# An FFT convolution with routed experts on one core: 48-point stages of groups 1 and 2 that are asked for sooner

## The chip, the core and the metric

The kernel runs on one core of a Trainium2 chip. A core has five engines with a program each, run in order: TensorE (PE; its weight loads are PEld), VectorE (DVE), ScalarE (ACT), GpSimd (POOL) and SyncE (SP), which issues most DMAs. An engine waits for another by semaphores, and what stands behind a waiting instruction on its engine waits too. 16 DMA engines move the data. The metric is the time of the device in microseconds; lower is better.

## The reference

`x` is 8 sequences of 5696 tokens of 128 numbers. Each channel is convolved causally with a filter `h` as long as the sequence (by a Fourier transform in the reference), and every token of the result goes to the one expert of eight with the largest logit:

```python
Yf = np.fft.rfft(x, n=2 * S, axis=1) * np.fft.rfft(h, n=2 * S, axis=0)[None]
y = np.fft.irfft(Yf, n=2 * S, axis=1)[:, :S, :].reshape(B * S, D)
logits = y @ w_gate
expert = np.argmax(logits, axis=1)
gate = softmax(logits)[expert]
for e in range(8):
    out[expert == e] = gate * (relu(y[expert == e] @ w1[e]) @ w2[e])
```

## The kernel before

**The convolution** is a transform in two factors: 119 points, padded to 120, by 48 points. The eight sequences go in three groups of 2, 3 and 3 (group 0, 1, 2), and each group passes three stages. Stage A (`steps_a`) makes the first factor: matmuls `pa`, copied to `ut` and stored to a buffer `VU` in DRAM. Stage B (`phase_b`), the 48-point stage, runs 120 items: an item is a forward matmul `xp`, a product with the filter's transform on VectorE (three instructions, `zt` and `xs`), a sum on GpSimd, and an inverse matmul `vp`, copied to `vt` and stored back to `VU`. Four items are a block, and a block needs four loads on SyncE: `mt` (forward matrices), `uq` (from `VU`, so all of stage A must be stored), two `mi` (inverse matrices) and two `hh` (filter). Blocks are asked for two ahead. Stage C (`phase_c`) makes the second factor (`yp`), transposes (`tp`), computes logits and gates (`lp`, `gb` and a chain of short VectorE instructions) and ranks tokens; GpSimd then sorts them by expert into a buffer `SR` with indirect DMAs. While group g is in stage C, group g+1's stage A runs as its guest.

**The experts** (`pipeline`) work on 185 tiles of 256 sorted tokens in four parts; part 0 has 26 tiles, part 1 has 33. A tile has four steps: in each a first-layer group `mh` of six matmuls, a ReLU `hs` on ScalarE and VectorE, and, two steps later, a second-layer group `ma`. A tile's tokens come as rows `xr` from `SR` and are transposed into `mx`; its weights come in four pieces `wb_0` to `wb_3` from `WD`. A piece is loaded in fact only where the expert changes, and in parts 0 and 1 there is one set of buffers, so a new expert's `wb_0` can only be loaded when the tile before has done with it. Rows are asked for by `usable(t)`, which wants the part sorted and the flag `state["alone"]` off; weights by `known(t)`, which wants the part's table.

**The order** of each engine's program comes from `run`: the streams (convolution, weight preparation, experts) are generators that yield a planned cost in ns, and the stream with the smallest planned time emits next. `STEP` (1420) is the planned cost of one expert step. `MIX_B`, `MIX_C`, `BESIDE` and `ENDING` say how many expert steps go with one item of stage B and one sub-step of stage C; `ENDING[g]` is that of the sub-steps after the last synthesis. In group 0 no experts run yet while `alone` is on. `next(after)` lets the next group's stage B emit its next piece: its first two pieces are requests of a block, further ones are items. `spin(n)` emits n filler matmuls on TensorE.

Of the kernel before, what the change touches and what calls it, by code (L numbers as in the profile page):

```python
# [49 lines left out]
MIX_B = (0.0, 0.45, 0.85)  # L50
MIX_C = (1.0, 1.2, 2.2)
BESIDE = (1.4, 1.2, 2.2)
ENDING = (1.4, 2.5, 2.5)
KNOWN = 2840
STAGED = 64
PAIRED = 2
# [3 lines left out]
HOLD = 3  # L60
FETCHED = (0, 1)
GUESTED = (0,)
EAGER = (2, 0)
SETTLED = (2840, 8000, 8000)
LEAD = (0, 4, 6)
A3 = (True, True, True)
# [4 lines left out]
LOGIT = (2, 2, 2)  # L71
RARE = 3
XR = 7
SPIN = (22, 40, 24)


@with_exitstack
def conv_moe(ctx: ExitStack, tc: tile.TileContext, I, out, B, S, D, E, F, split):
# [73 lines left out]
    groups, parts = [], []  # L152
# [74 lines left out]
    def spin(count):  # L227
        bank = ps.tile([P, 512], F32, tag="cx", name=f"spin{spun[0]}", bufs=4)
        spun[0] += 1
        for k in range(count):  # L230
            nc.tensor.matmul(
                bank, fcr[:, 0, 0], fcr.rearrange("p a c q -> p (a c q)"), start=True, stop=True
            )
# [220 lines left out]
    def phase_b(gr, guest=None):  # L454
# [139 lines left out]
        if g == 0:  # L594
            spin(SPIN[0])
        for qb in range(2 if g == 0 else 0):
# [42 lines left out]
    state = {"w9": [const.tile([MP, max(SLOTS), E1], F32, name=f"w9{k}") for k in range(2)]}  # L639
# [51 lines left out]
    def phase_c(gr, guest=None, after=None):  # L691
        g, nb, cb, cw, NI, ns = gr.g, gr.nb, gr.scb, gr.scw, gr.ni, gr.ns
# [9 lines left out]
        nu = NB // NI  # L702
# [16 lines left out]
        def bank(name, tag):  # L719
            return ps.tile([P, 512], F32, tag=tag if state["alone"] else "cx", name=name, bufs=banks[tag] if state["alone"] else 4)  # L720
# [178 lines left out]
        finished, ahead = [None], [0]  # L899
# [4 lines left out]
        for n in range(n_end + 1):  # L904
            for k in range(nsub):
                at = n * nsub + k
                if parts[0].ready and state["prepped"]:
                    state["alone"] = False
                if k == 0:
                    load(n + 2)  # L910
                made = turning = read = carried = None
                if n < nu:
                    made = synth(n, k)
                if TL <= at < total_sub + LL:
                    tp = bank(f"tp{g}_{n}_{k}", "ma")
                if 0 <= at - TL < total_sub:
                    turning = turn(*divmod(at - TL, nsub), tp)
                whole = 0 <= at - LL < total_sub and (at - LL) % nsub == nsub - 1
                if whole:
                    for j in range(nsub):  # L920
                        spare = tp if j else ybank.get((n, k))
                        if spare is None:
                            spare = bank(f"lp{g}_{n}_{k}", "mh")
                        read = logit((at - LL) // nsub, j, spare)
                if k == 0 and n >= sl:
                    score(n - sl, n - sl - 1)
                if guest:
                    few = n < QUIET[g] or k == 0 and n >= sl and not state["alone"] and g
                    carried = guest.begin(1 if few else 2)
                ties = [made, read, carried] if carried and read else [made, turning, read or carried]  # L930
                ties = [x for x in ties if x is not None]
                count = 3 if len(sorts) > 8 else PER_SUB[g]
                for x in ties if len(ties) <= count else ties[:1] + ties[len(ties) - count + 1 :]:
                    sort_one(x)
                if state["alone"]:
                    yield cost if n < nu else cost / 2
                else:
                    yield STEP * (BESIDE if n < nu else ENDING)[g]
                if guest:
                    guest.end()  # L940
                    if guest.m >= guest.M and not guest.over and guest.done():
                        finished[0] = at
                if finished[0] is not None and at >= finished[0] + 4 and n >= nu - EAGER[g] and ahead[0] < 2:
                    next(after)
                    ahead[0] += 1
                if n < nu:
                    divide(*divmod(at + AHEAD, nsub))
                    settle(n, k)
                if 0 <= at - TL < total_sub:
                    turned(*divmod(at - TL, nsub))  # L950
                for j in range(nsub if whole else 0):
                    logit_out((at - LL) // nsub, j)
                if k == 0:
                    chains = []
                    if 0 <= n - sl - 1 < nu:
                        chains.append(rank(n - sl - 1))
                    if 0 <= n - sl < nu:
                        chains.append(route(n - sl))
                    zipped(*chains)
                    if n - sl - 1 in closes:  # L960
                        pt = closes[n - sl - 1]
                        chores.append(tables(pt, state["base"]))
                        if pt is parts[-1]:
                            chores.append(fill(pt, state["base"]))
                chore(3 if state["alone"] is False else 10)
                if at >= total_sub + LL:
                    break
        if guest:
            if not guest.over:
                yield from guest.rest()  # L970
            state["spare"] = g > 0
        state["alone"] = False
        more = True
# [129 lines left out]
    def home(t):  # L1103
        return seq[t][1] % sets(t)
# [159 lines left out]
    def pipeline(lo, hi):  # L1264
        LAG = 2
        step, nrow, nw, turned = (lo, 0), lo, (lo, 0), lo
        seen, hist, passed = {}, [None] * (LAG + 1), {}
        while True:
            t, k = step
            while nw[0] < min(t + 3, hi) and known(nw[0]):  # L1270
                was, n = user[nw[0]], nw[1]
                if home(nw[0]) and not state["spare"]:
                    break
                if was is not None and was >= lo and passed.get((was, n // 2), -1) < 2 * (n % 2) + 1:
                    break
                load_w(nw[0], n)
                nw = (nw[0], n + 1) if n < 3 else (nw[0] + 1, 0)
            while nrow < min(t + 4, hi) and usable(nrow):
                load(nrow)
                seen[nrow] = len(hist)  # L1280
                nrow += 1
            act = step if t in xts and nw > (t, k // 2) else None
            hist.append(act)
            old, done = hist[-1 - LAG], hist[-2 - LAG]
            to = done[0] if done and done[1] == NPAIR - 1 else None
            ti = turned if turned < nrow and seen[turned] + 2 <= len(hist) else None
            if ti is not None and (act and k < LAG or ti > t + 1 or act is None and ti > t):
                ti = None
            if act is None and old is None and to is None and ti is None:
                state["acting"] = False  # L1290
                leave(len(hist))
                recall(len(hist))
                deliver()
                if t >= hi and not (any(hist[-1 - LAG :]) or pending or leaving or staged or coming or returned):
                    return
                busy = pending or leaving or staged or coming or returned or turned < nrow or any(hist[-1 - LAG :])
                yield STEP if busy else None
                continue
            leave(len(hist))
            recall(len(hist))  # L1300
            if act and step == (0, 0):
                spin(SPIN[2])
            if act:
                layer1(t, k)
                state["acting"] = True
                passed[t, 0] = k
            if ti == 0:
                spin(SPIN[1])
            if to is not None or ti is not None:
                turn(to, ti)  # L1310
            if old:
                layer2(*old)
                passed[old[0], 1] = old[1]
            yield STEP
            done = None
            if act:
                done = relu(t, k)
                step = (t, k + 1) if k < NPAIR - 1 else (t + 1, 0)
                if k == NPAIR - 1:
                    xts.pop(t)  # L1320
            if ti is not None:
                turned_in(ti)
                turned += 1
            if old and old[1] == NPAIR - 1:
                drain(old[0])
            if to is not None:
                emit(to, len(hist))
            deliver(done)
# [140 lines left out]
```

## Time and profile before

| | us |
|---|---|
| median of 3 runs (2144.11 to 2147.92) | 2147.75 |
| the profiled execution, its own time | 2146.88 |
| its span, first to last instruction | 2145.2 |
| TensorE busy in the span | 2052.4 (96%) |
| VectorE busy | 1556.4 (73%) |
| GpSimd busy | 1264.6 (59%) |
| ScalarE busy | 1104.5 (51%) |

Busy shares are means over stages with different limits. Stage A and B of group 0 fill the time to some 260 us, its stage C that to some 400; experts and convolution then run together to some 1600, and experts alone from there. Matmuls are pipelined, so a few in a row start closer together than their durations say, and some matmul records are missing, which shows as idle time that no wait explains.

### The profile page before, as it was taken

Reading aid. Unit: us, or ns where it says so; the run is one execution under the profiler, and the core shown is the slowest. Engines: PE = TensorE matmul, PEld = TensorE weight load, DVE = VectorE, ACT = ScalarE, POOL = GpSimd, SP = SyncE. Lnnn points to the kernel's source line nnn. Section 1 sums busy time; section 2 is a strip of 40 time slices with the busy share of each in tenths; the row PEclk is TensorE's granted clock in tenths of the full one; section 3 lists DMA queues with packets and bytes.
Section 4 is the critical chain, followed back from the end, with each engine's and each line's share of the span. In section 5 each row is a group of like instructions: output and inputs, shape, how many; then the busy total and the mean of one; then the engine's idle time right before and its main releaser. Section 6 shows DMA issues by size and latency. Waiting matters only on the chain.

```text
span 2145.2 us, 47047 instructions
## 1 busy us (share of the span) xinstructions
PE 2052.4 (96%) x14284; PEld 1763.9 (82%) x14284; DVE 1556.4 (73%) x3731; ACT 1104.5 (51%) x2359; POOL 1264.6 (59%) x1399
## 2 busy tenths in 40 slices
PE   7899899899999999989999999999999999999998
PEld 5788666666667988876777779999989999999998
DVE  3598856699987788879988885777765555555554
ACT  5688755233334666633443345655544444554544
POOL 5366547565653388882665661788876444444443
PEclk9999999999999999999999999999999999999999
DMA  9899999799997788767889886666645543444441
GB/s 340 291 301 325 320 395 366 213 278 279 272 279 234 288 273 296 264 198 218 250 249 248 243 246 228 212 209 211 199 149 186 170 139 108 142 138 143 143 144 34
DMA packets 236901, 494.39 MB, mean 230 GB/s; under 512 B 33553, under 2 KB 146446, under 8 KB 236647
## 3 DMA queue, kind: packets, MB, share of 16 engines
q1 hardware_dynamic: 212279, 443.06, 66.2%
q0 software_dynamic: 24368, 48.29, 6.9%
q8 instruction: 116, 1.90, 0.4%
q14 instruction: 138, 1.13, 0.2%
HBM read 598.31 MB, written 176.80 MB: 361 GB/s over the span
## 4 chain that ended last, share of the span: by engine, by line
PE 29%; issue 15%; POOL 13%; DMA 6%; DVE 6%; ACT 1%; SPq 1%; POOLq 1%; DVEq 0%; ACTq 0%
PE mh L1164 9%; PE ma L1185 8%; POOL out L1240 8%; POOL SR L656 3%; PE vp L564 3%; PE xp L528 3%; PE yp L742 2%; DMA SR<-rt,pi 2%; DMA wb<-WD 2%; POOL c_fcs L650 1%; PE mx L183 1%; DVE hs L1172 1%; PE pa L315 1%; PE tp L183 1%; DMA vq<-VU 1%
## 5 line engine op out<-in xcount | busy, mean ns | idle before, releaser
L1172 DVE SCALAR_TENSOR_TENSOR hs<-mh,hs 128x512 fp32r<-128x512 f32 x728 | 501.4, 691 | 371.6 <-ACT hs L1170 366.5
L1164 PE MATMUL mh<-xtb,wb 128*128 128x256 f32 x4368 | 686.0, 293 | 27.2 <-DMA wb<-WD 12.7
L1170 ACT ACTIVATE hs<-mh 128x512 fp32r<-128x512 f32 x728 | 435.7, 599 | 449.3 <-PE mh L1164 435.4
L1164 PEld LDWEIGHTS mh<-xtb,wb 128*128 128x128 f32 x4368 | 582.8, 189 | 95.3 <-issue 34.3
L1185 PE MATMUL ma<-hs,wb 128*128 128x256 f32 x4368 | 653.7, 285 | 7.3 <-DMA wb<-WD 7.3
L1185 PEld LDWEIGHTS ma<-hs,wb 128*128 128x128 f32 x4368 | 566.9, 190 | 8.7 <-DMA wb<-WD 8.7
L656 POOL DMA_INDIRECT SR<-rt,pi x384 | 402.8, 1049 | 196.3 <-issue 55.0
L1240 POOL DMA_INDIRECT out<-xr x250 | 243.8, 975 | 316.0 <-DVE xr L1203 257.7
L555 POOL TENSOR_TENSOR zt<-zt,xs 128x384 f32<-128x384 f32 (+1 forms) x280 | 298.3, 1075 | 115.3 <-DVE xs L547 86.9
L579 ACT COPY vt<-vp 96x384 f32<-96x384 f32 (+1 forms) x300 | 149.1, 497 | 349.2 <-PE vp L564 344.4
L564 PE MATMUL vp<-zt,mi 128*96 128x384 f32 (+1 forms) x720 | 259.2, 455 | 7.2 <-DVE xs L547 5.8
L528 PE MATMUL xp<-uq,mt 96*128 96x384 f32 (+1 forms) x720 | 258.7, 454 | 4.4 <-ACT vt L579 2.3
L540 DVE TENSOR_TENSOR zt<-xp,hh 128x384 f32<-128x384 f32 (+1 forms) x300 | 174.0, 580 | 54.6 <-PE xp L528 40.6
L564 PEld LDWEIGHTS vp<-zt,mi 128*96 128x96 f32 x720 | 113.3, 163 | 100.2 <-issue 52.1
L1240 POOL DMA_INDIRECT out<-xb x114 | 111.1, 975 | 135.3 <-ACT hs L1170 111.0
L547 DVE SCALAR_TENSOR_TENSOR xs<-xp,hh 64x384 f32<-64x384 f32 (+1 forms) x300 | 175.7, 586 | 6.1
L545 DVE TENSOR_TENSOR xs<-xp,hh 64x384 f32<-64x384 f32 (+1 forms) x300 | 173.2, 577 | 6.0
L315 PE MATMUL pa<-xc,fcr 120*128 120x512 f32 x576 | 166.8, 420 | 11.0 <-ACT xc L293 4.0
L528 PEld LDWEIGHTS xp<-uq,mt 96*128 96x128 f32 x720 | 121.7, 192 | 34.7 <-issue 13.1
L315 PEld LDWEIGHTS pa<-xc,fcr 120*128 120x128 f32 x576 | 101.5, 192 | 44.5 <-DVE rk L867 7.5
L650 POOL TENSOR_TENSOR c_fcs<-c_fcs 120x64 f32<-120x64 f32 (+1 forms) x288 | 125.9, 437 | 6.2
L742 PE MATMUL yp<-vr,gcr 120*120 120x384 f32 x576 | 117.5, 338 | 1.2 <-DVE vr L730 1.1
(137 smaller groups left out, 2275.6 us busy)
## 6 DMA issues: line engine op xcount, KB each, us to landing
wb<-WD SPq DMA_DIRECT2D x728, 512.0 KB
vq<-VU SPq DMA_DIRECT2D x64, 768.0 KB
VU<-ut SPq DMA_DIRECT2D x48, 768.0 KB
uq<-VU SPq DMA_DIRECT2D x60, 576.0 KB
VU<-vt SPq DMA_DIRECT2D x60, 576.0 KB
xt<-x SPq DMA_DIRECT2D x96, 256.0 KB
xr<-SR SPq DMA_DIRECT2D x182, 130.0 KB
hh<-HS SPq DMA_DIRECT2D x120, 192.0 KB
```

The source lines that it names most:

```text
L315: done = nc.tensor.matmul(banks[m], lhs, rhs, start=(k == 0), stop=(k == len(ops) - 1))
L528: nc.tensor.matmul(xj, mt[:, k0 + j, :], uc.rearrange("p (b d) -> p b d", d=D), start=True, stop=True)
L540: nc.vector.tensor_tensor(out=zt, in0=x3, in1=hv[:, 0].broadcast_to([P] + wide), op=ALU.mult)
L547: nc.vector.scalar_tensor_tensor(out=xs[to], in0=x3[at], scalar=-1.0, in1=him, op0=ALU.mult, op1=ALU.mult)
L555: eng.tensor_tensor(out=zt, in0=zt, in1=xs, op=ALU.add)
L564: nc.tensor.matmul(vp[:K2, j * cw : (j + 1) * cw].rearrange("p (b d) -> p b d", d=D), mi[:, k0 + j, :], zt.rearrange("p b (j d) -> p b j d ...
L656: s = nc.gpsimd.indirect_dma_start(out=SR[:, :], out_offset=IndirectOffsetOnAxis(ap=pi[:, b : b + 1], axis=0), in_=rt[:, b, :], in_offset= ...
L1164: nc.tensor.matmul(hp[:, u, :], wb[:, a, f, :], xt[:, b, :], start=(n == 0), stop=(n == 2))
L1170: done = nc.scalar.activation(hs[:, 0], hp, AF.Relu)
L1172: nc.vector.scalar_tensor_tensor(out=hs[:, 1], in0=hp, scalar=0.0, in1=hs[:, 0].bitcast(F32), op0=ALU.max, op1=ALU.subtract)
L1185: nc.tensor.matmul(accs[t], wb[:, a, f, :], hs[:, b, u, :], start=(k == 0 and u == 0 and n == 0), stop=(k == NPAIR - 1 and u == 1 and n == 2),
L1240: sc = nc.gpsimd.indirect_dma_start(out=out[:, :], out_offset=IndirectOffsetOnAxis(ap=xr[:, s, D + 1 : D + 2].bitcast(I32), axis=0), in_=x ...
```

## The change

`EAGER` and the third number of `SPIN` go. In group 0's stage C, `alone` stays on until the stage ends. The next group's two block requests are made as soon as stage A of that group has ended (group 0), or one sub-step after that among the ending sub-steps (group 1); for group 0 every further sub-step then also emits an item of stage B, with 40 fillers ahead of the first. The 40 fillers ahead of tile 0's rows and the 24 ahead of tile 0's first step go. `ENDING` of group 1 is 1.4 where it was 2.5.

```diff
-ENDING = (1.4, 2.5, 2.5)
+ENDING = (1.4, 1.4, 2.5)
-EAGER = (2, 0)
-SPIN = (22, 40, 24)
+SPIN = (22, 40)
@@ phase_c, each sub-step
-                if parts[0].ready and state["prepped"]:
+                if g and parts[0].ready and state["prepped"]:
                     state["alone"] = False
...
-                if finished[0] is not None and at >= finished[0] + 4 and n >= nu - EAGER[g] and ahead[0] < 2:
-                    next(after)
-                    ahead[0] += 1
+                if finished[0] is not None and n >= nu * g and at >= finished[0] + g:
+                    if ahead[0] < 2:
+                        for _ in range(1):
+                            next(after)
+                            ahead[0] += 1
+                    elif g == 0:
+                        if ahead[0] == 2:
+                            spin(SPIN[1])
+                        ahead[0] += 1
+                        yield next(after)
...
             if not guest.over:
                 yield from guest.rest()
+            while ahead[0] < 2:
+                next(after)
+                ahead[0] += 1
@@ pipeline
-            if act and step == (0, 0):
-                spin(SPIN[2])
             if act:
                 layer1(t, k)
...
-            if ti == 0:
-                spin(SPIN[1])
```

Line numbers differ by one to nine between the two kernels. What the change does to the order shows at three places. On SyncE, where group 1's stage B begins: the last store of its stage A, and what is requested behind it. Before:

```order
L308 DMA VU_71<-ut_11_1_4309 128x1536
...
L1115 DMA xr_4467<-SR 128x260
...
L1115 DMA xr_4500<-SR 128x260
...
L1135 DMA wb_0_4511<-WD 128x1024
...
L464 DMA mt_0_4761<-mq 96x512
L472 DMA uq_0_4763<-VU_71 96x4x384
L475 DMA mi_98<-miq 48x384 x2
L479 DMA hh_95<-HS 48x1024 x2
```

And after the change:

```order
L307 DMA VU_71<-ut_11_1_4309 128x1536
L463 DMA mt_0_4439<-mq 96x512
L471 DMA uq_0_4441<-VU_71 96x4x384
L474 DMA mi_98<-miq 48x384 x2
L478 DMA hh_95<-HS 48x1024 x2
...
L1144 DMA wb_0_4569<-WD 128x1024
...
L1144 DMA wb_3_4575<-WD 128x1024
...
L478 DMA hh_97<-HS 48x1024 x2
...
L1124 DMA xr_4685<-SR 128x260
```

The first block has moved from behind the rows and weights of tile 0 to directly behind the stores; left out between `hh_95` and `wb_0` is the second block (item 4 on), between `wb_3` and `hh_97` the third (item 8 on) but for that line. The rows of tiles 0 to 3, which came first, now come behind three blocks and four weights.

On TensorE, at the same place, from the fillers on. Before:

```order
L231 MATMUL spin_4519<-fcr 128x512 x40
L183 MATMUL mxNone_4560<-ident,xr_4467 128x128 x2
L782 MATMUL lp_16_1_4596<-yt_15_4440,c_small 32x120 x3
L782 MATMUL tp_16_1_4595<-yt_15_4440,c_small 32x120 x3
L231 MATMUL spin_4609<-fcr 128x512 x24
L1164 MATMUL mh_0_4634<-xtb_4606,wb_0_4511 128x256 x6
...
L1185 MATMUL ma_4698<-hs_2_4739,wb_3_4517 128x256 x6
L528 MATMUL xp_0_0_4824<-uq_0_4763,mt_0_4761 128x384
```

And after the change:

```order
L781 MATMUL tp_16_1_4506<-yt_15_4448,c_small 32x120 x3
L230 MATMUL spin_4517<-fcr 128x512 x40
L527 MATMUL xp_0_0_4558<-uq_0_4441,mt_0_4439 128x384
...
L527 MATMUL xp_6_0_4740<-uq_4_4468,mt_4_4466 128x384
L563 MATMUL vp_2_0_4742<-zt_2_0_4661,mi_98 96x384
L182 MATMUL mxNone_4751<-ident,xr_4685 128x128 x2
L527 MATMUL xp_7_0_4763<-uq_4_4468,mt_4_4466 128x384
L563 MATMUL vp_3_0_4765<-zt_3_0_4671,mi_98 96x384
L527 MATMUL xp_8_0_4777<-uq_8_4652,mt_8_4586 128x384
L563 MATMUL vp_4_0_4779<-zt_4_0_4730,mi_99 96x384
L1173 MATMUL mh_0_4791<-xtb_4788,wb_0_4569 128x256 x6
```

Items 0 to 6 forward and 0 to 2 back now stand ahead of the transposes of tile 0's rows (`mxNone`), and items 7 and 8 ahead of its first step. The item that stood level with tile 1's first step (`xp_0`) now comes a tile and a quarter sooner in the order.

On SyncE, where group 2's stage B begins (`VU_72`). Before, the piece `wb_0` of tile 34 comes behind the first block:

```order
L1216 DMA STG<-xr_11791 128x260
L464 DMA mt_0_13172<-mq 96x512
L472 DMA uq_0_13174<-VU_72 96x4x384
L475 DMA mi_98<-miq 48x384 x2
L479 DMA hh_95<-HS 48x1024 x2
L1135 ISA
L1135 DMA wb_3_4517<-WD 128x1024
...
L1135 DMA wb_0_4511<-WD 128x1024
```

And after the change, where the pieces are those of tile 30, but for `wb_3`, which is tile 29's:

```order
L307 DMA VU_72<-ut_11_1_12235 128x1536
L1225 DMA STG<-xr_10926 128x260
...
L1144 DMA wb_3_4575<-WD 128x1024
...
L1144 DMA wb_0_4569<-WD 128x1024
L463 DMA mt_0_12662<-mq 96x512
L471 DMA uq_0_12664<-VU_72 96x4x384
L474 DMA mi_98<-miq 48x384 x2
L478 DMA hh_95<-HS 48x1024 x2
L1144 ISA
L1144 DMA wb_1_4571<-WD 128x1024
L1144 ISA
L1144 DMA wb_2_4573<-WD 128x1024
```

The first block has moved some three tiles ahead, close behind the last stores of stage A, and it now stands between the first and the second weight piece of a tile.

## Rows read from the trace of the kernel before

**Rows 1.** Stretches: us, busy us (instructions) PE PEld DVE ACT POOL, PEclk, DMA share, GB/s.

```profile
450.00:500.00 50.00, 49.46 (x245) 33.83 (x244) 48.37 (x90) 18.91 (x42) 30.79 (x31) 1.00 1.00 275
900.00:950.00 50.00, 41.57 (x345) 38.36 (x344) 36.61 (x151) 24.07 (x60) 43.39 (x63) 0.95 0.69 218
1700.00:1750.00 50.00, 50.00 (x431) 50.00 (x430) 28.16 (x50) 24.82 (x49) 24.42 (x26) 1.00 0.45 148
```

**Rows 2.** Timeline of TensorE: start, us, line, operation, out<-in, count [idle before <-releaser].

```profile
388.00 9.36 PE L231 MATMUL spin<-fcr 120*128 120x512 f32 x40
397.20 0.43 PE L183 MATMUL mxNone<-ident,xr 128*128 128x128 f32 x2
398.11 5.76 PE L231 MATMUL spin<-fcr 120*128 120x512 f32 x24
412.47 0.81 PE L528 MATMUL xp<-uq,mt 96*128 96x384 f32 x2
421.11 0.88 PE L528 MATMUL xp<-uq,mt 96*128 96x384 f32 x2 [2.16 <-DMA uq<-VU]
...
429.67 0.81 PE L528 MATMUL xp<-uq,mt 96*128 96x384 f32 x2
430.31 0.81 PE L564 MATMUL vp<-zt,mi 128*96 128x384 f32 x2
```

**Rows 3.** Timeline of SyncE's DMA issues: start, us, line, out<-in, count.

```profile
386.63 2.08 SPq L308 DMA_DIRECT2D VU<-ut  x2
394.99 3.76 SPq L1115 DMA_DIRECT2D xr<-SR  x4
399.55 6.89 SPq L1135 DMA_DIRECT2D wb<-WD  x5
...
406.88 0.44 SPq L472 DMA_DIRECT2D uq<-VU  x1
```

**Rows 4.** Shorter stretches at the first start, columns as in rows 1.

```profile
388.00:430.00 42.00, 38.19 (x211) 30.11 (x210) 24.15 (x84) 8.64 (x20) 22.44 (x23) 0.96 0.88 233
392.00:394.00 2.00, 2.00 (x10) 1.68 (x9) 0.00 (x0) 0.00 (x0) 1.60 (x2) 1.00 0.48 158
402.00:406.00 4.00, 3.52 (x24) 2.86 (x23) 0.00 (x0) 0.60 (x1) 0.00 (x0) 1.00 1.00 386
408.00:422.00 14.00, 11.14 (x71) 8.81 (x70) 12.57 (x44) 4.02 (x9) 7.74 (x9) 1.00 1.03 234
422.00:426.00 4.00, 4.00 (x16) 3.34 (x15) 3.26 (x7) 0.48 (x1) 2.47 (x3) 0.57 1.00 237
```

**Rows 5.** The page's DMA issues: out<-in, queue, count, size of one.

```profile
wb<-WD SPq DMA_DIRECT2D x728, 512.0 KB
...
uq<-VU SPq DMA_DIRECT2D x60, 576.0 KB
...
hh<-HS SPq DMA_DIRECT2D x120, 192.0 KB
mt<-mq SPq DMA_DIRECT2D x90, 192.0 KB
...
mi<-miq SPq DMA_DIRECT2D x120, 72.0 KB
```

**Rows 6.** VectorE's groups, 430 to 650: count | busy us, mean ns | idle before.

```profile
L547 DVE SCALAR_TENSOR_TENSOR xs<-xp,hh 64x384 f32<-64x384 f32 x103 | 57.6, 559 | 1.9
L540 DVE TENSOR_TENSOR zt<-xp,hh 128x384 f32<-128x384 f32 x103 | 57.0, 553 | 8.2 <-PE xp L528 6.4 <-DMA hh<-HS 0.2
L545 DVE TENSOR_TENSOR xs<-xp,hh 64x384 f32<-64x384 f32 x103 | 56.7, 551 | 1.9
```

**Rows 7.** Second start: the longest wait of TensorE, SyncE's issue, the stretch behind.

```profile
PE mh L1164 <- DMA wb<-WD: 7.6, 1, 7.6
939.80 4.54 SPq L1135 DMA_DIRECT2D wb<-WD  x4
949.00:955.00 6.00, 5.96 (x28) 5.99 (x29) 1.70 (x5) 1.57 (x3) 5.17 (x9) 0.50 1.08 261
```

## The prediction, made before the run

> **What bounds the kernel now.** First I read the span in stretches of 50 us [rows 1]. The matmul stream sets the time: from 1700 on TensorE is 100% busy, and with the 48-point items running (450 to 500) it still is 99%, although VectorE is 97% busy and the DMA engines are full (share 1.00). All engines run their programs in order, so the total is TensorE's work plus the time in which it stands still or runs at half clock. A tile that the change puts off is not lost: it is done in the tail at the same price. So I cost the change by what TensorE fills its time with at the two places where a 48-point stage begins: near 390 (group 1) and near 930 (group 2; 900 to 950 has 8.4 us without a matmul).
>
> At the first place the timeline shows two blocks of filler matmuls, 9.36 and 5.76 us, and the first item only at 412.47, which stands in the order behind five first-layer groups of tiles 0 and 1 [rows 2]. SyncE issues the last stores of the first stage by 388.7, then the rows of tiles 0 to 3, then weights, and only at 406.88 the first block of the 48-point stage [rows 3]. At the second place TensorE waits 7.6 us for weights, which stood behind the first block's requests, and then runs 6 us at a granted clock of 0.50 [rows 7].
>
> **The first start, term by term.** *Removed:* the 24 fillers, 5.76 us on TensorE. In 388 to 430 TensorE is busy 38.19 of 42 us, so 3.8 us of waits go too, and 422 to 426 at a granted clock of 0.57 cost 4 x 0.43 = 1.7 [rows 4]. Together 11.3 us that the changed order need not pay.
>
> *Added:* waits of another kind. By the order, SyncE now has behind the stores: block 0, block 4, the four weights of tile 0, block 8, and then the rows of tiles 0 to 3. TensorE has: filler 40, items 0 to 6 forward, items 0 to 2 back, and then the transposes of tile 0's rows, which everything later stands behind. Two times have to be found: when TensorE comes there, and when the rows land.
>
> TensorE: lp and tp (0.6) go ahead of the fillers, which so end at 388.0 + 0.6 + 9.4 = 398.0. The load of uq_0 must wait for the stores: they are issued by 388.7 [rows 3], and in 392 to 394 the DMA share is down to 0.48 [rows 4], so I take 393.6 for their landing. Until then SyncE stands, with everything behind it. A load takes 1.7 us beyond its bytes: the first rows, 130 KB (0.55 us at 234 GB/s), were issued at 394.99 and used at 397.20 [rows 2, 3]. Sizes [rows 5]: uq 576 KB, two mi of 72, two hh of 192, mt 192. Block 0's 1104 KB at 234 GB/s are there at 393.7 + 1.7 + 4.8 = 400.2. VectorE makes an item in 553 + 551 + 559 = 1663 ns [rows 6]. Item 6 needs the bank that item 4's product frees, and vp of item 2 comes right behind: 400.2 + 5 x 1.66 + 2 x 0.65 = 409.8, call it 410 (0.65 us is the distance of xp and vp at 429.67 and 430.31 [rows 2]). In those 12 us TensorE does 10 x 0.65 + 0.6 of gates: 4.9 us empty.
>
> The rows: ahead of them, their own 130 KB (128 x 260 numbers) counted, lie 1104 + 1296 + 2048 + 1296 + 130 = 5874 KB, 6.0 MB. How fast they move the trace shows only for neighbours: 386 GB/s while the weights come (402 to 406), 234 GB/s while blocks of this stage come (408 to 422, DMA share 1.03) [rows 4]. With 2.1 MB of weights at 386 and 3.9 MB of the rest at 234: 5.4 + 16.7 = 22.1 us, landing at 393.7 + 1.7 + 22.1 = 417.5. All at 386 would give 411.0, all at 234 421.1; I take the mixture, since each row is of the same transfer that it prices. So the wait at the transposes is 7.5 us (1 to 11). After a standstill of 7.6 us the clock was at 0.50 for 6 us [rows 7], which costs 3; and since the items between the first steps of tile 0 come two or three to a step, VectorE binds a little: 1.
> The Trainium skill ("DMA: Bandwidth & Descriptors", Specifications) has about 358 GB/s as HBM's limit for a core; by that rate alone the 6.0 MB would be there at 412.2 and this start would end 3.3 us ahead. The stretch 408 to 422 does not bear it out (234 GB/s with the engines full), and that of the weights goes beyond it (386 GB/s), so the rows decide.
>
> Sum of the first start: 4.9 + 7.5 + 3 + 1 - 11.3 = **+5.1** (from 4.9 + 1 + 0 + 1 - 11.3 = -4.4 to 4.9 + 11 + 3 + 1 - 11.3 = +8.6). The fillers that stay are free in either case: they lie under the stores' landing and the first load.
>
> **The second start.** *Removed:* the sub-steps behind group 1's last synthesis get fewer expert steps (ENDING 2.5 to 1.4), and the blocks are asked for earlier, so the stage starts some 3 tiles earlier in the order. Worked out from the inputs, the expert changes before tiles 30, 34, 38. Before, the change at 34 fell on the first block's requests: 7.6 us of waiting and 3 us of clock [rows 7], 10.6 in all. *Added:* now the change at tile 30 falls there. Its first weights go ahead of block 0, the next two behind it, with mt, uq, mi and hh between. From mt_0's request to their use lie nine groups of six matmuls (50 us hold 431 matmuls in the tail [rows 1], so 0.7 us a group: 6.3) and transposes, gates and logits, which I estimate at 3.5: about 9.8 us. Against that stand the wait of uq_0 for the last stores (they need 393.6 - 388.7 = 4.9 us, and are asked for only some 2 us before: about 3), then 1.13 MB at 234 (4.8), 1.05 MB of weights at 386 (2.7) and 1.7: 12.2 us. That is a wait of 2.4; the first weights, behind those 1.5 MB of stores, may come 1 to 2 us late as well. I take 4 us of waiting and 2 of clock: **-4.6** (from no wait, -10.6, to the same wait as before, 0).
>
> **The rest.** `alone`, kept until group 0's sort ends, is what holds tile 0's rows back behind three blocks (counted above), and the forced second request only makes sure of what the order shows; LEAD and the tail are untouched. Weight changes elsewhere shift by 2 to 4 tiles against the items and may wait more or less there: 0, plus or minus 3. Two to four more tiles in the tail cost what they cost elsewhere.
>
> Sum: +5.1 - 4.6 + 0 = +0.5 on the profiled execution's own 2146.9 us (span 2145.2 and 1.7 around it): 2147.4. The median of the runs shown is 0.9 above that execution, so I forecast **2148.3**.
>
> **Rivals.**
> *Loads at the weights' rate* (faster). If blocks that come without the experts' traffic move at 386 GB/s, the rows land at 411 and TensorE hardly waits: -4.4 - 4.6 = -9, **2139**. For it: in 408 to 422 other traffic shared the engines. Against: blocks have shorter pieces than weights, and the engines were full. The Trainium skill's limit named above speaks for this side.
> *Everything at the blocks' rate* (slower). At 234 GB/s throughout the rows land at 421.1 (+8.6), and at the second start the weights need 1.8 us more (-4.6 becomes about -2): +6.6, **2155**. It decides from the point where tile 0's rows land later than 420. For it: the DMA engines stay full through the whole stage [rows 1]. Against: the weights did move faster.
> *The early start does nothing* but drop fillers: both starts stay as long as they were in waits, -5.8, **2142.5**. Against: the first item moves ahead of tile 0 in the order, so the waits must change.
>
> **How the numbers follow.** What a measurement can tell from no change is about 0.2%, 4.3 us. Chances: the forecast and what lies within 4.3 us of no change 0.37; loads at the weights' rate 0.28; everything at the blocks' rate 0.31; fillers alone 0.04. So faster 0.32, the same 0.37, slower 0.31. The range takes in both main rivals, with half the 3 us of the rest beyond the slower one: 2139 to 2157. The forecast's own range is 2144 to 2152.
>
> **What would show it.** Right: the first item at 398 to 400; a wait of 5 to 10 us of TensorE on tile 0's rows near 410 to 418, released by the load from SR, with half clock behind it; the 7.6 us wait for weights at the second start gone, two or three shorter ones near tile 30 in its place. Wrong, if the rows are there when TensorE comes (faster), if the transposes wait over 10 us or the second start still has a wait of 7 us (slower), or if weights wait longer in places that I put at 0.

## The result

The changed kernel takes **2168.4 us** (median of 4 runs, 2166.84 to 2169.52), the kernel before 2146.27 (4 runs): a ratio of **1.0117**, 95% interval 1.0100 to 1.0133. The forecast was 2148.3, range 2139 to 2157. The profiled execution's span grew from 2145.2 to 2167.9 us, by 22.7.

In what follows, what TensorE **loses** in a stretch is the time in which it stands still and half of the time in which it is busy at a granted clock of 0.50, the lower of its two levels (1.2 of 2.4 GHz). The stretches of the changed kernel (columns as in rows 1): the 60 us from the 40 fillers on, 76 us around its second start, the 100 us around the last item of group 2's 48-point stage, parts of these, and the tail:

```profile
390.00:450.00 60.00, 46.84 (x195) 29.53 (x190) 41.59 (x113) 11.49 (x28) 34.70 (x35) 0.89 1.01 258
406.00:413.00 7.00, 5.44 (x10) 2.54 (x10) 6.52 (x33) 0.24 (x1) 1.49 (x2) 0.51 1.03 339
419.00:426.00 7.00, 2.70 (x6) 1.68 (x7) 1.99 (x5) 0.00 (x0) 4.03 (x4) 0.56 0.87 230
912.00:988.00 76.00, 63.12 (x356) 49.72 (x355) 58.13 (x164) 22.41 (x51) 41.75 (x64) 0.87 0.81 220
1216.00:1316.00 100.00, 90.30 (x548) 75.07 (x547) 66.66 (x119) 39.13 (x79) 47.44 (x48) 0.93 0.72 214
1700.00:1750.00 50.00, 50.00 (x431) 50.00 (x430) 28.14 (x50) 24.84 (x49) 24.35 (x26) 1.00 0.46 148
```

And the same places of the kernel before, which rows 1 and 4 do not hold:

```profile
388.00:448.00 60.00, 55.60 (x290) 41.14 (x289) 41.13 (x115) 15.26 (x35) 34.95 (x36) 0.97 0.95 244
926.00:1002.00 76.00, 64.18 (x408) 51.99 (x408) 62.39 (x171) 25.79 (x55) 39.53 (x59) 0.93 0.73 194
1220.00:1320.00 100.00, 98.98 (x651) 82.93 (x650) 76.98 (x139) 47.12 (x97) 50.91 (x52) 1.00 0.82 254
```

Read them so: in 390 to 450 TensorE stands 60 - 46.84 = 13.2 us, and half of its busy time at half clock (most of it in the next two rows) is 4.4, 17.6 in all. The places then lose:

| | before | after | difference |
|---|---|---|---|
| first start, 60 us | 6.1, and 5.8 of the 24 fillers | 17.6 | +5.7 |
| second start, 76 us around the first item | 14.8 | 21.6 | +6.9 |
| end of that stage, 100 us, without tile 53's change of expert | 1.0 | 10.3 | +9.3 |
| tile 53's change of expert, 12 us | 2.1 | 5.5 | +3.4 |
| everywhere else, by difference to the span (500 to 700 loses 11.3 before, 4.6 after) | | | -2.6 |

The 100 us of the changed kernel lose 15.8 in all. But 5.5 of that is a change of expert before tile 53, which comes beside items in both kernels. In the kernel before it lies just outside the 100 us, so it has a line of its own (before, then after):

```profile
1208.97 0.98 PE L1185 MATMUL ma<-hs,wb 128*128 128x256 f32 x6 [2.11 <-DMA wb<-WD]
1238.56 1.23 PE L1173 MATMUL mh<-xtb,wb 128*128 128x256 f32 x6 [3.77 <-DMA wb<-WD]
```

The tail has its 431 matmuls in 50 us as in rows 1: the tiles that were put off cost no more there. VectorE's item instructions take 553, 551 and 560 ns, as in rows 6.

**First start**, TensorE (compare rows 2), VectorE's first product and then SyncE (rows 3):

```profile
390.48 9.36 PE L230 MATMUL spin<-fcr 120*128 120x512 f32 x40
400.93 0.88 PE L527 MATMUL xp<-uq,mt 96*128 96x384 f32 x2 [1.09 <-DMA uq<-VU]
407.56 0.23 PE L803 MATMUL gb<-oh,ones 120*128 120x54 bf16 x1 [4.79 <-DVE rk L866]
423.30 0.69 PE L182 MATMUL mxNone<-ident,xr 128*128 128x128 f32 x2 [6.51 <-DMA xr<-SR]
```

```profile
403.72 0.56 DVE L539 TENSOR_TENSOR zt<-xp,hh 128x384 f32<-128x384 f32 x1 [11.48 <-DMA hh<-HS]
```

```profile
387.98 1.78 SPq L307 DMA_DIRECT2D VU<-ut  x2
389.81 0.71 SPq L463 DMA_DIRECT2D mt<-mq  x1
394.81 0.32 SPq L471 DMA_DIRECT2D uq<-VU  x1
403.11 4.51 SPq L1144 DMA_DIRECT2D wb<-WD  x4
414.74 6.83 SPq L1124 DMA_DIRECT2D xr<-SR  x4
```

SyncE stands at `uq` for 4.3 us until the stores are through (390.52 to 394.81), and the rows, behind all that, are issued at 414.74 instead of 394.99. From 394.8 to 423.3, when TensorE gets the rows, the engines moved 246 GB/s on the mean.

**Second start**, TensorE and SyncE (rows 7). Tile 30's four weight pieces are late one after the other, 10.6 us in four waits where there was one of 7.6 (the two `wb` issues at 913.31 are tile 29's last piece and tile 30's first):

```profile
922.37 1.62 PE L1173 MATMUL mh<-xtb,wb 128*128 128x256 f32 x6 [4.49 <-DMA wb<-WD]
930.21 0.94 PE L1173 MATMUL mh<-xtb,wb 128*128 128x256 f32 x6 [1.64 <-DMA wb<-WD]
932.07 1.65 PE L1194 MATMUL ma<-hs,wb 128*128 128x256 f32 x6 [0.48 <-DMA wb<-WD]
940.59 1.65 PE L1194 MATMUL ma<-hs,wb 128*128 128x256 f32 x6 [4.01 <-DMA wb<-WD]
```

```profile
909.72 0.87 SPq L307 DMA_DIRECT2D VU<-ut  x2
910.64 0.96 SPq L1225 DMA_DIRECT2D STG<-xr  x1
913.31 3.18 SPq L1144 DMA_DIRECT2D wb<-WD  x2
916.53 1.28 SPq L463 DMA_DIRECT2D mt<-mq  x1
...
920.65 2.07 SPq L1144 DMA_DIRECT2D wb<-WD  x2
```

The first piece's issue ends at 916.49 and TensorE uses it at 922.37, 5.9 us later. The stores were through by then: the engines moved 54 GB/s from 916 to 918. In the 4 us behind that they moved some 1.2 MB, more than twice the piece, so part of the block requested right behind it came along with it:

```profile
916.00:918.00 2.00, 1.88 (x21) 1.49 (x15) 1.80 (x8) 0.73 (x3) 1.80 (x3) 1.00 0.40 54
918.00:920.00 2.00, 0.00 (x0) 0.00 (x0) 0.59 (x1) 0.17 (x2) 1.78 (x4) 1.00 0.92 356
920.00:922.00 2.00, 0.00 (x0) 0.00 (x0) 0.00 (x0) 0.00 (x0) 1.59 (x4) 0.90 1.02 226
```

**End of the stage.** The last item stands level with tile 56.5 of the order, before with 60.0. Part 2 of the tiles begins at 59 with a new expert, and its weights, which came beside items before, are now needed where experts run without items beside them; TensorE waits there twice:

```profile
1297.24 1.62 PE L1173 MATMUL mh<-xtb,wb 128*128 128x256 f32 x6 [2.38 <-DMA wb<-WD]
1305.18 1.62 PE L1173 MATMUL mh<-xtb,wb 128*128 128x256 f32 x6 [3.41 <-DMA wb<-WD]
```

Half clock behind them adds 4.4 us, which makes 10.3 with the waits. The third wait in these 100 us, 3.8 us at 1238.56, is the one for tile 53's weights, and half clock behind it costs 1.7.

### The profile page after: what moved, and what is told of

Same layout as the page of the kernel before. It is cut to its first block, busy times and chain, and to the rows that moved or that the text cites. A ratio compares the mean times of both kernels' runs of the same rounds, so it can differ in the third digit from the quotient of the medians.

```text
span 2167.9 us, 47003 instructions
## 1 busy us (share of the span) xinstructions
PE 2059.5 (95%) x14260; PEld 1767.8 (82%) x14260; DVE 1555.1 (72%) x3731; ACT 1105.8 (51%) x2359; POOL 1270.2 (59%) x1399
## 5 line engine op out<-in xcount | busy, mean ns | idle before, releaser
L1194 PEld LDWEIGHTS ma<-hs,wb 128*128 128x128 f32 x4368 | 570.1, 191 | 10.4 <-DMA wb<-WD 10.2
L655 POOL DMA_INDIRECT SR<-rt,pi x384 | 407.6, 1061 | 199.5 <-issue 50.0
```

The lines of the kernel that those rows point to most:

```text
L655: s = nc.gpsimd.indirect_dma_start(out=SR[:, :], out_offset=IndirectOffsetOnAxis(ap=pi[:, b : b + 1], axis=0), in_=rt[:, b, :], in_offset= ...
L1194: nc.tensor.matmul(accs[t], wb[:, a, f, :], hs[:, b, u, :], start=(k == 0 and u == 0 and n == 0), stop=(k == NPAIR - 1 and u == 1 and n == 2),
```

## The experiments

They ran on four other chips, on which the kernel before takes 2183 to 2199 us, so each is given as its ratio to the kernel before on the same chip. The change itself was not timed on these; the run with two late loads below (1.0114) is almost the same program. The theory after reading the two traces was that of three separate accounts: the first start, the second start, and changes of expert that now fall elsewhere against the items.

**The two parts apart.** Group 0's part alone (ENDING of group 1 and its request condition as before), and group 1's part alone:

```diff
-ENDING = (1.4, 1.4, 2.5)
+ENDING = (1.4, 2.5, 2.5)
-                if finished[0] is not None and n >= nu * g and at >= finished[0] + g:
+                if finished[0] is not None and n >= nu * g and at >= finished[0] + 4 * g:
```

> The first start's part alone: items of group 1's 48-point stage among the last sub-steps, fillers moved, rows held back; ENDING of group 1 stays 2.5 and its block requests stay where they were. In the trace of the change TensorE loses 18.6 us (standing still or at half clock) in 387 to 450 where it lost 6.1 before, and 5.8 us of fillers are gone: net +6.7. Theory (three accounts: first start, second start, weight changes that fall elsewhere against the items): this part by itself also puts group 2's 48-point stage 2.25 tiles sooner in the order (at tile 32.5, before 34.75), so that it pays the first start, +7, and part of the other two: between 2151 and 2163, more than the first start explains. Rival (each part pays for its own start alone): the first start and nothing else, 2153, with the second start's 7.6 us wait as before. Rival (the whole loss sits in group 1's part): no change, 2146.

> The second start's part alone: ENDING of group 1 at 1.4 and its block requests one sub-step behind the guest's end; group 0's stage and its fillers as before. The stage then begins at tile 33.5 of the order (before 34.75, with the whole change 31.25). Theory (three accounts): what it costs depends on where the changes of expert fall, here the one before tile 34 right behind the first block; without the first start's 6.7 us it is between 2142 and 2156, and together with the first part's cost it need not add up to the change's 22 us. Rival (each part pays for its own start alone): 22 minus 7, thus 2161.

Measured: 1.0086 (1.0056 to 1.0116) and 1.0045 (1.0021 to 1.0069), that is +19 and +10 us, both at or just beyond the upper end of what the theory allowed. Of "each pays for its own start" the +7 falls, and the +15 lies at the very edge of its interval; the two parts together exceed the change's 22 us. That group 1's part holds the whole loss falls too. The stretch around the end of the stage in the one and the other, where it ends at tile 57.75 and 58.75:

```profile
1256.00:1356.00 100.00, 90.88 (x557) 74.72 (x556) 66.93 (x122) 40.52 (x83) 46.26 (x46) 0.95 0.69 214
1264.00:1364.00 100.00, 94.38 (x598) 79.05 (x599) 69.69 (x126) 42.33 (x86) 45.82 (x46) 0.97 0.70 216
```

**No loads of weights at changes of expert**, in the kernel before and in the changed one (`in1=ej[:, back:]` where the table compares with the tile before, so that the flag is 0).

> The kernel before, with the flag in the table that loads a tile's weights at a change of expert set to 0: each part keeps its first expert's weights, so the output is not the reference's; every other instruction and the order stay. In the trace of before TensorE waits 20 us for weight pieces in all and runs at half clock behind the longest of these waits (about 5 us lost). Theory: these go, 2118 to 2128. Rival (the places would wait for something else anyway, blocks or rows): 2135 or more.

> The changed kernel with the same edit (no loads of weights at changes of expert; output not the reference's). Theory (three accounts): the second start and the shifted weight changes cost nothing any more, and only the first start stays: 5 to 9 us above the kernel before with the same edit. Rival (an earlier 48-point stage costs by its own blocks and items, not by weights): still 15 to 22 us above it. Rival (lost fillers, that is clock alone): 2 to 4 us above it.

Measured: 0.9938 (0.9919 to 0.9957) and 0.9987 (0.9964 to 1.0009): -14 and -3 us, about 11 apart. The first lies between what its theory and its rival allowed, and is less than the 20 us of waits: part of them came back as others (the second start still loses 15.1). Of the change's 22 us about half goes with these loads, where the theory had all but the first start's 5 to 9 us go. The edit leaves the first tiles of each part, which always load, and there the two kernels still differ (the end of the stage in before and in the changed kernel, both with the edit):

```profile
1247.00:1347.00 100.00, 99.50 (x656) 83.60 (x655) 77.41 (x139) 47.19 (x96) 50.41 (x51) 1.00 0.71 215
1225.00:1325.00 100.00, 93.14 (x583) 77.04 (x582) 72.65 (x131) 42.61 (x87) 50.89 (x51) 0.97 0.67 203
```

That pointed to part 2's first tiles: 0.5 us is lost there in the kernel before and 9.5 in the changed one, and tile 53's change loads nothing in either. The second start loses 15.1 and 18.8 even without loads: most of what a second start costs is not weights. The 3.7 us between these two are half clock (3.4 and 7.5) at about equal standstill (11.6 and 11.3); what makes them was not tried.

**What holds up tiles 59 and 60.** In the change's order two loads of the third stage (`vq`, 1536 KB) stand between the first and second piece of tile 59. One kernel asks for them three steps later:

```diff
+        late = 3 if g == 2 else 0
+        if late:
+            yield STEP * late
         for i in range(0 if guest and g == 0 else 2):
             load(i)
         if g:
-            yield STEP * LEAD[g]
+            yield STEP * (LEAD[g] - late)
```

> The changed kernel, and group 2's third stage asks for its first two loads (1536 KB) three planned steps later, so that they stand behind the weights of tiles 59 and 60 and not between the first and the second piece of tile 59. Nothing else moves. In the trace of the change the 100 us around that place hold 15.8 us of standstill and half clock, before 1.0. Theory (collision of conv loads and weight pieces): 8 to 14 us faster than the change, ratio to the kernel before 1.005 to 1.008. Rival (the eight pieces of tiles 59 and 60 are late by themselves, since both sets are loaded at once): within 3 us of the change, 1.010 to 1.012.

Measured: 1.0114 (1.0088 to 1.0139), and those 100 us lose 15.9. The rival held: these two loads are not what makes the weights late. The other kernel keeps the order of loads and lengthens the stage: `MIX_B` of group 2 is 0.97 for 0.85.

> The changed kernel with MIX_B of group 2 at 0.97 (0.85): more expert steps go with an item, so that group 2's 48-point stage ends at tile 60.0, as in the kernel before, and not at 56.5; its start stays. Six kernels so far show, in the 100 us around the end of that stage, 1.0, 1.3, 0.9 us of standstill and half clock where it ends at tile 60, 8.6 and 9.0 at 58.75, 14.0 at 57.75, 15.8 and 16.0 at 56.5. Theory (cover): the weights of tiles 59 and 60, eight pieces, are hidden only beside items; behind the stage's end experts run bare and wait. Then these 100 us fall to 1 to 3 us and the kernel is 8 to 14 us faster than the change: ratio 1.005 to 1.008. Rival (the loss belongs to the earlier start of the stage, and only shows there): the loss stays or moves into the stage, 1.010 to 1.013.

Measured: 1.0042 (1.0021 to 1.0063), about 16 us off the change, somewhat more than expected. The 100 us at the stage's end, and the 249 us of the stage ahead of them:

```profile
1263.00:1363.00 100.00, 99.87 (x672) 85.12 (x671) 76.82 (x137) 48.30 (x97) 51.81 (x52) 1.00 0.79 249
1014.00:1263.00 249.00, 238.43 (x1368) 184.34 (x1367) 208.45 (x380) 99.44 (x202) 136.76 (x136) 0.97 0.83 235
```

0.1 us is lost at the end, at the price of some more inside the stage (18.3 us; 11.8 in the 228 us of the change). The 100 us of the expectation take in tile 53's change of expert where the stage ends early. From 25 us ahead of the last item to 35 us behind it, which leaves that out, the fifteen kernels that load these weights lose 0.1 to 1.3 us where the stage ends at tile 60, 4.6 and 4.9 at 58.75, 6.6 at 57.75 and 9.3 to 12.9 at 56.5 (10.2 in the change). So this loss, the largest account, goes with where the stage ends, whatever moved it. That the items cover the loads of tiles 59 and 60 is the reading that fits. Items do not hide every load: tile 53's waits beside them.

**The order at the second start.** Requests later, so that three of tile 30's four pieces go ahead of the first block:

```diff
-                if finished[0] is not None and n >= nu * g and at >= finished[0] + g:
+                if finished[0] is not None and n >= nu * g and at >= finished[0] + 4 * g:
```

> The changed kernel, and group 1's block requests come four sub-steps behind the guest's end, not one: three of the four pieces of tile 30's weights now stand ahead of the first block, the fourth behind it. Items and experts keep their places in the order. Theory (a block between the pieces): the four waits of the change at its second start (4.5, 1.6, 0.5 and 4.0 us) and their half clock shrink, 75 us there lose 14 to 17 instead of 21.6: ratio 1.008 to 1.010. Rival (the ending sub-steps have too little other work for any change of expert, whatever the order): 1.011 to 1.013, with the waits moved from weights to item 0's data.

Measured: 1.0073 (1.0048 to 1.0098); the second start loses 15.1 us instead of 21.6:

```profile
931.00:1007.00 76.00, 64.84 (x392) 49.50 (x390) 62.44 (x186) 25.28 (x57) 44.90 (x68) 0.93 0.84 230
```

```profile
937.51 2.22 SPq L1144 DMA_DIRECT2D wb<-WD  x2
943.25 0.95 PE L1173 MATMUL mh<-xtb,wb 128*128 128x256 f32 x6 [1.29 <-DMA wb<-WD]
```

The theory held, with a little more gained than expected. Tile 30's first piece (the second issue of this row) has the same stores ahead of it but no block behind it, and is used 3.5 us behind its issue. In the kernel with the longer stage, on the same chip and with the change's order, that took 5.6 us. So a block costs both where it stands between the pieces and where it follows the first at once. Without weights the change still loses 3.7 us more here (above), so weights need not be all of it. The same step in the kernel before (`finished[0] + (1 if g else 4)`, which there puts two blocks ahead of tile 34's pieces):

> The kernel before, and only group 1's block requests come one sub-step behind the end of its guest instead of four. The 48-point stage of group 2 stays at tiles 34.75 to 60; its first two blocks now stand ahead of the four pieces of tile 34's weights and the third behind them. Theory (what costs is a block between the pieces, not the early request): the 7.6 us wait of before and its half clock shrink to 3 us or less, 5 to 10 us faster, ratio 0.995 to 0.998. Rival (earlier blocks hold the weights up just the same): ratio 0.999 to 1.002.

Measured: 0.9993 (0.9976 to 1.0009); no wait over 1.2 us there is put down to a weight any more, but these 76 us lose 16.1, and another long wait stands in its place, at tile 34's first step:

```profile
976.79 1.62 PE L1164 MATMUL mh<-xtb,wb 128*128 128x256 f32 x6 [4.50 <-DVE rk L867]
```

Whether it is VectorE's chain or again a weight (a wait for several semaphores is put down to the last) stays open; this matmul reads `xtb` and `wb` and not `rk`, which speaks for a weight. The time is the rival's, and the theory missed. An earlier request by itself gained nothing.

**Rows ahead at the first start.** `if parts[0].ready` instead of `if g and parts[0].ready`, alone and with ENDING of group 1 at 2.5:

> The changed kernel, with the flag that holds back the rows of tiles 0 to 3 taken off where the kernel before takes it off, so that the rows and the first weights are requested ahead of the blocks. Item 0 still comes among the last sub-steps. The second start falls at tile 33.5 (31.25 in the change), the end of that stage at 58.75 (56.5), as in the run of the second part alone. Theory (three accounts): the 6.5 us wait of the transposes for rows goes, and the piece order at tile 30 and at tile 59 is not met any more: 12 to 20 us below the change, a ratio to the kernel before of 0.999 to 1.006. Rival (lost fillers and clock at the first start): the wait moves to item 0's data or to weights, and the first start still costs 6 us or more: 1.006 to 1.010.

> The changed kernel with the rows ahead of the blocks as above and ENDING of group 1 back at 2.5: early requests in both groups, but the stage of group 2 at tiles 34.75 to 60 as in the kernel before. Theory (three accounts): the first start costs 0 to 3 us, the second start less than before, and nothing collides at tile 59: ratio 0.994 to 0.999, the best so far. Rival (the first start's early items cost by lost fillers and clock, whatever the rows do): 1.000 to 1.004.

Measured: 1.0101 (1.0077 to 1.0125) and 1.0066 (1.0043 to 1.0090); both expectations missed. The edit did less and more than was expected of it. It put the rows only ahead of the second block, still behind SyncE's wait at `uq`, and it moved tile 0's transposes ahead of the fillers (the first of the two kernels):

```profile
424.63 0.69 PE L182 MATMUL mxNone<-ident,xr 128*128 128x128 f32 x2 [14.09 <-DMA xr<-SR]
```

With the 40 fillers put ahead of these transposes again:

```diff
+            if ti == 0:
+                spin(SPIN[1])
             if to is not None or ti is not None:
                 turn(to, ti)
```

> The changed kernel with the rows of tiles 0 to 3 ahead of the blocks, the 40 fillers ahead of tile 0's transposes, as in the kernel before, and ENDING of group 1 at 2.5. In the run of the rows ahead without this the transposes stood ahead of the fillers and waited 14 us for the sort to end, since rows can be read only then. What is left of the change is item 0 earlier by a tile and a quarter, early requests and no 24 fillers. Theory (the change's first start loses by rows behind three blocks): the first start now costs no more than in the kernel before, ratio 0.997 to 1.000. Rival (items ahead of tile 0's steps cost by themselves, through VectorE's order behind item 0): 1.002 to 1.005.

Measured: 1.0015 (0.9994 to 1.0036), between the two theories. TensorE still waits 4.45 us for rows, since the first block's `uq` stands ahead of them and itself waits for the stores. SyncE in this kernel, and below in the kernel before without the 24 fillers, where rows follow the stores:

```profile
416.01 2.08 SPq L307 DMA_DIRECT2D VU<-ut  x2
418.15 0.51 SPq L463 DMA_DIRECT2D mt<-mq  x1
423.58 0.31 SPq L471 DMA_DIRECT2D uq<-VU  x1
...
427.11 3.79 SPq L1122 DMA_DIRECT2D xr<-SR  x4
```

```profile
410.76 2.08 SPq L308 DMA_DIRECT2D VU<-ut  x2
415.24 4.06 SPq L1115 DMA_DIRECT2D xr<-SR  x4
```

So one block ahead of the rows is enough to hold them up: 11.1 us from the first store to the rows instead of 4.5.

**The 24 fillers**, taken out of the kernel before:

> The kernel before without the 24 fillers (5.76 us) ahead of tile 0's first step. The prediction counted them as 5.8 us that the change saves. If they lie on the path: 5 to 6 us faster, ratio 0.9970 to 0.9976. If they only fill a wait that would be there without them (the weights of tile 0 are requested at 399.55, the fillers end at 403.87): ratio 0.999 to 1.001, and the wait for weights grows by what the fillers took. If they keep the clock up: slower, 1.001 to 1.003.

Measured: 0.9982 (0.9963 to 1.0001), 4 us but not clear of no change, and between what the expectations allowed. In the 60 us from the 40 fillers on, this kernel loses 8.3 us, and the two below without the 24 fillers 9.3 each. The four traces that have them and the first start of before lose 6.1 (before), 3.3, 3.7 and 5.9 (on other chips), and 5.8 of fillers. So of 5.8 us between nothing and 3.6 are won, 1.5 by the means, and how much of the fillers lies on the path is not settled.

**The sum.** Both repairs in the change; the kernel before without fillers and with early requests; and group 1's part on the kernel without fillers, its end put back by `MIX_B` 0.89:

> The changed kernel with both repairs at once, MIX_B of group 2 at 0.97 and requests four sub-steps behind the guest's end; only the first start is left as in the change. Alone they gave 1.0042 and 1.0073 where the change has 1.0117. Theory (first start, order at the second start and cover at the stage's end are separate accounts): the first start's 6 to 9 us remain, less 3 to 4 us for the 24 fillers that are gone: ratio 1.001 to 1.004. Rival (a fourth account, for instance weight changes inside the longer stage): 1.005 or more. If the repairs add up in full, 0.9998.

> The kernel before without the 24 fillers and with group 1's requests one sub-step behind the guest's end. Alone these gave 0.9982 (interval 0.9963 to 1.0001) and 0.9993. If they add up: 0.9975, clear of no change. If the 24 fillers' gain was noise: 0.999 to 1.000.

> Group 1's part of the change on the kernel before without the 24 fillers, and with the stage's end put back to tile 60.0 by MIX_B 0.89: ENDING of group 1 at 1.4, requests one sub-step behind the guest's end, stage from tile 33.5 to 60.0. The part without these repairs gave 1.0045. Theory (the loss of that part is cover at the stage's end and changes of expert that fall among its blocks): with the end repaired, the 100 us there lose 1 us where they lost 8.6, ratio 0.998 to 1.001, so that the earlier stage by itself is worth nothing. Rival (an earlier stage is a gain once it collides with nothing): 0.994 to 0.997.

Measured: 1.0018 (1.0002 to 1.0034), 0.9972 (0.9952 to 0.9992), 1.0020 (1.0000 to 1.0041). With both repairs 4 us remain, which is less than the change loses but not the full sum of 0.9998. The first start there loses 15.0 where the old one loses 3.3 to 6.1 and 5.8 of fillers, 3.1 to 5.9 more. So the three accounts make up the loss within what these runs can tell. The second is the one version that is clear of the kernel before, and it is what its two parts add up to; which of them gains is not settled. In the third, just above what the theory allowed, the end of the stage loses 0.2 us, but the 238 us of the stage ahead of it 19.6. There 13.0 of 14.5 us of standstill are put down to weights (4.5 of 7.8 in the 218 us of the kernel before):

```profile
PE mh L1164 <- DMA wb<-WD: 7.4, 4, 3.2
PE ma L1185 <- DMA wb<-WD: 5.6, 3, 3.5
```

Why weights are late beside items in a stretched stage was not tried. An earlier second stage was worth nothing in either run that tried it without the first start's part.

## Why the prediction was wrong

- **What bounds it** (TensorE's work, standstill and half clock; the tail takes tiles at the same price): right.
- **First start, +5.1**: right, +5.7, though in part by terms that made up for each other. First item at 400.93 (forecast 398 to 400). Empty ahead of the rows 1.09 + 4.79 + 0.57 = 6.5 us (4.9): the long one is a matmul of the gates, `gb`, that waits for `rk`. VectorE's order has item 0's product ahead of `rk`, and that waited until 403.72 for block 0's `hh` (the working has block 0 there at 400.2). The wait for rows is 6.51 (7.5), but its two ends both moved by 6 to 7 us, which is luck: the rows came at 423.3 and not at 417.5, TensorE at 416.8 and not at 410. That landing is past even the 421.1 of blocks' rate throughout; the stores landed at 394.8 and not at 393.6, the mean rate from there was 246 GB/s where the mixture has 272, and SyncE came to issue the rows only at 414.74. Half clock 4.4 (3). The 24 fillers were counted as 5.8 saved; the runs do not show more than 3.6 of it when they go alone.
- **Second start, -4.6**: the first step that failed, "4 us of waiting and 2 of clock". It measured 10.6 and 8.8, +6.9 against before. The working followed two pieces, `wb_1` and `wb_2`, and allowed the first 1 to 2 us for the 1536 KB of stores ahead of it. That piece came 4.5 late, though the stores were through when it was issued: block 0 was requested right behind it. The fourth, not looked at, came 4.0 late, behind the second block. The 3 us that `uq_0` was to wait for the stores did not arise: SyncE issued it at 917.93, 8 us after them, having stood at the first piece. With the four waits came three stretches at a granted clock of 0.50 (6.8, 3.4 and 10.2 us), where the kernel before had one of 10.2. The run with requests four sub-steps behind the guest's end, which loses 15.1, shows that the order of requests makes this difference.
- **The rest, 0 plus or minus 3**: the second step that failed, by 10 us where the first failed by 11.5. The shift by 2 to 4 tiles was seen, but only where the stage begins; it moves the stage's end too, from tile 60.0 to 56.5, past the change of expert at 59. +9.3 there, +3.4 at tile 53 and -2.6 elsewhere make +10.1. The experiment with the longer stage, which puts the end back to tile 60 and loses 0.1 us there, shows that it is the end that was left out.
- **Rivals**: "everything at the blocks' rate" named the right sign and, for the first start, the right mechanism (rows later than 420, at 246 GB/s), but its 2155 lacked the two terms above. Its 2155 and the 2142.5 of the fillers alone are also added to the forecast and not to the kernel before, which makes them 0.5 too high, and the stores' landing is 393.6 in the text and 393.7 in the sums; none of these decides anything.

## What to carry to other kernels

When a change moves one stream of work against another, look at both ends of the moved stage: which loads lose the work that hid them is as much a term of the sum as what the new start waits for. Price a moved request by everything behind it in its queue, and follow every piece of a set of loads, not the first two. Where requests wait for stores in an in-order queue, what is needed next goes ahead of them.

## What the runs showed of the hardware

One stage takes longer on the other chips, with the same program. Here is the kernel before, and below it the run with early requests on a chip where before takes 2183 us; the two have the same order up to 350 us:

```profile
0.00:260.00 260.00, 238.04 (x1277) 192.84 (x1278) 180.59 (x265) 185.67 (x346) 147.40 (x129) 0.98 0.94 316
300.00:350.00 50.00, 48.54 (x290) 33.45 (x282) 34.03 (x166) 28.91 (x74) 39.03 (x37) 1.00 1.03 380
```

```profile
0.00:260.00 260.00, 237.26 (x1278) 192.68 (x1279) 180.71 (x266) 185.62 (x347) 147.51 (x129) 0.98 0.94 317
300.00:350.00 50.00, 41.48 (x231) 27.87 (x230) 26.81 (x142) 21.90 (x57) 33.17 (x32) 0.93 0.92 329
```

Stages A and B of group 0 are equal; in stage C, with its many short instructions on all engines, TensorE is busy 41.5 of 50 us instead of 48.5. All fifteen runs on the four other chips have 38.7 to 41.5 us there, the two on the first chip 48.3 and 48.5. Where the kernels have the same order up to the 40 fillers, these start at 388.0 on the first chip and between 412 and 423 on the others, which is most of the 37 to 53 us between the chips. Why was not tried. And half clock costs only what is done in it: in 419 to 426 the granted clock is 0.56, but TensorE is busy for 2.70 us and loses 1.3 by it; 406 to 413, as long and at 0.51, costs 2.7.
